# A fused attention and feed-forward kernel: a new order for its first seven chunks and its last four passes

## The chip, the core and the metric

The kernel runs on one core of a Trainium2 chip. A core has TensorE (PE, with its weight loads PEld), VectorE (DVE), ScalarE (ACT), GpSimd (POOL) and SyncE (SP), each with a queue of its own that it works off in order, and 16 DMA engines that they share. The metric is the time of one execution in device microseconds, the median of several runs.

## The reference

For 8 batches, 8 heads, 576 positions and head width 64, with a decay g = 1 - 2^(-5-h) of head h, and the feed-forward part on all 4608 tokens:

```python
scores = scale * np.matmul(q, k.transpose(0, 1, 3, 2))
Dmat = np.where(rel >= 0, gamma[:, None, None] ** rel[None, :, :], 0.0)
ret = scores * Dmat[None, :, :, :]
x = np.matmul(ret, v)            # then heads side by side: 4608 x 512
...
h = x @ w_in                     # 512 x 1024
e = np.exp(h - h_max)
sm = e / (np.sum(e, axis=-1, keepdims=True) + 1e-09)
solu = h * sm
mu = np.mean(solu, axis=-1, keepdims=True)
var = np.mean((solu - mu) ** 2, axis=-1, keepdims=True)
ln = (solu - mu) / np.sqrt(var + 1e-06) * g_ln
return ln @ w_out                # 1024 x 512
```

## The kernel before

The tokens are cut into 36 chunks of 128 rows. Chunks come in four groups of nine: the four full chunks of two batches, alternating, then one chunk that holds the last 64 positions of both. The decay is folded into q and v, so attention is causal linear attention: within a chunk a masked product, between chunks a running state per batch.

A step is a small function that issues one chunk's share of work on one engine. A token such as `eq:2:a` in a string means step `eq` for chunk base + 2, on ACT (`v` is DVE, `g` is POOL). The steps are, in the order in which a chunk goes through them:

- `ld`: three loads (q, k, v; 256 KB each) on SP. `cq`, `ck`, `cv`: q, k, v to 16 bits, q and v scaled.
- `tq`: 8 transposes of q and k into PSUM (PE); `eq`: their copy to SBUF. `sc`: scores (PE); `mk`: the mask on them (DVE, two instructions).
- `kv`: the chunk's share of the state (PE); `ad`: added to the state (DVE); `dk`, `d3`: decayed copies (POOL).
- `av`, `fs`: the attention's output from within the chunk and from the state (PE); `ex`: its copy (xT).
- `m1`: h = x w_in, eight products of 128x512 (PE), or in four pieces `mr` of two. `mx`: the row maximum (DVE); `xp`: the exponential (ACT); `so`: h times it and its sum, into u (DVE); `ce`: mean taken off (DVE); `sq`: sum of squares (ACT); `rt`: one over the root (POOL).
- `tu`: 8 transposes of u (PE); `eu`: their copy uT. `m2`: eight products with w_out (PE). `st`: scaling on ACT and the store on SP.

`li` and `lo` load w_in and w_out in four pieces each, `wi` and `wo` convert them in eight. The steps that begin with h do the last chunk in halves. `wu:0:n` issues n products of a tile of zeros, 128x512, into a PSUM tile that nobody reads.

Nothing is planned at run time: the string START is issued, then LOOP once for each i from FIRST on, then END, and each engine works its instructions off in that order, waiting on semaphores where an operand or a buffer isn't ready. Before, FIRST is 4, LOOP runs for i = 4 to 34, and END does the rest. One pass of LOOP carries m1 of chunk i, m2 of chunk i - 2, scores of chunk i + 2 and loads of chunk i + 6. In PSUM, h has a ring of two; all other tiles share four banks, which the string BANKS deals out in the order of their allocation, so that a step can wait for the reader of another tile that held its bank before.

Of the kernel before, what the change touches and what calls it, by code (L numbers as in the profile page):

```python
# [16 lines left out]

FIRST = 4  # L20
START = """
c1:0 ld:1 li:3 ld:0 ck:0:v li:2 li:1 cq:1:g li:0 cv:1:v ck:1:a cq:0:g wu:0:8 tq:1 ld:3 wu:0:15
kv:1 wi:2:0:v wi:0:0:a eq:1:v ld:2 tq:0 wi:1:1:g cv:0:v wi:3:1:a wu:0:6 sc:1 eq:0:v wi:3:0:a
mk:1 wu:0:3 sc:0 ld:4 kv:0 wi:1:0:v c2:0 lo:0 ad:1 ck:3:a wu:0:1 av:1 ad:0 lo:3 wi:2:1:a mk:0
cq:3:g fs:1 dk:1 tq:3 ex:1:a dk:0 d3:1 wu:0:2 mr:1:3 cq:2:g eq:3:a d3:0 cv:3:v lo:1 mr:1:2
cv:2:g lo:2 ck:2:a wi:0:1:v av:0 kv:3 mr:1:0 sc:3 fs:0 ld:5 cq:4:g ad:3 tq:2 mr:1:1 mk:3
ex:0:a mr:0:2 mr:0:1 kv:2 av:3 mx:1 eq:2:a sc:2 ad:2 dk:3 d3:3 cv:4:g d3:2 mk:2 mr:0:0 mr:0:3
av:2 fs:3 mx:0 fs:2 xp:1 dk:2 wo:0:g ck:4:a ex:2:a tq:4 wo:4:g so:1 kv:4 wu:0:2 m1:2 xp:0
eq:4:a so:0 ce:0 ld:6 wu:0:1 tu:0 ld:7 cq:5:g ce:1 ld:8 ex:3:a ad:4 wo:7:a wo:6:a wo:3:a
wo:2:v sq:1 sc:4 mx:2 m1:3 tu:1 wo:1:a mk:4 eu:0:v av:4 xp:2 wo:5:a ck:5:g cv:5:v tq:5 fs:4  # L30
eq:5:v sq:0 eu:1:a mx:3 rt:1 m2:0 rt:0 cq:6:g so:2 m2:1 st:0 ex:4:a cq:7:g sc:5 ck:6:v cv:6:g
ce:2 xp:3 ld:9 st:1 mk:5 ck:7:g
"""
LOOP = """
tu:-2 so:-1 tq:2 dk:0 d3:0 eq:2:a eu:-2:a ce:-1 m1:0 kv:1 ad:1 av:1 sc:2 mx:0 sq:-2 mk:2 fs:1
ex:1:a rt:-2 cq:4:g xp:0 ld:6 m2:-2 st:-2 cv:3:v ck:4:g
"""
END = """
sq:-2 tu:-2 hm:0:0 eu:-2:a so:-1 ce:-1 hx:0:0 hm:0:1 hx:0:1 hp:0:1 tu:-1 hp:0:0 m2:-2 eu:-1:v
ho:0:1 rt:-2 ho:0:0 m2:-1 sq:-1 rt:-1 hc:0 ht:0:0 hq:0:0:a ht:0:1 hq:0:1:v he:0:0:a st:-2  # L40
he:0:1:v st:-1 h2:0:0 rt:0 h2:0:1 hw:0:0:a hw:0:1:v
"""

BANKS = """
012302210201313202132013203200310210302312032103210231023120312032103213021302310231032103213021
302310231032103213021302310231032103201320130213021032103201320130213021032103201320130213021032
10312031201320132103210312031201320132103210312031201320132013231001
"""


# [25 lines left out]
def kernel(  # L76
# [38 lines left out]
    NCH = len(chunks)  # L115
# [37 lines left out]
    def ld(n):  # L153

        for key, src in (("qf", q), ("kf", k), ("vf", v)):
            dst = load.tile([P, H, D], FP, name=key)
            for pp, b, s0 in rows(n):
                m = pp.stop - pp.start
                nc.sync.dma_start(  # L159
                    out=dst[pp], in_=src[b, :, s0 : s0 + m, :].rearrange("h p d -> p h d")  # L160
                )
            T[key, n] = dst

    def scaled(n, key, out, table, engine):
        dst = half.tile([P, H, D], F16, name=out)
        engine.tensor_tensor(  # L166
            out=dst, in0=T.pop((key, n)), in1=table.unsqueeze(2).to_broadcast([P, H, D]),
            op=ALU.mult,
        )
        T[out, n] = dst  # L170
# [48 lines left out]
    def mk(n):  # L219

        i = 1 if chunks[n][1] == 4 else 0
        m = tris[:, i : i + 1].to_broadcast([P, 4, P])
        T["ret", n] = []
        for e, s in enumerate(T.pop(("sc", n))):
            r = att.tile([P, 4, P], F16, name=f"ret{e}")
            nc.vector.tensor_tensor(out=r, in0=s, in1=m, op=ALU.mult)  # L226
            T["ret", n].append(r)

# [126 lines left out]

    def so(n):

        u = moe.tile([P, DFF], F16, name="u")
        su = tiny.tile([P, 1], FP, name="su")
        nc.vector.scalar_tensor_tensor(  # L360
            out=u, in0=T.pop(("h", n)), scalar=1.0, in1=T.pop(("e", n)), op0=ALU.mult,
            op1=ALU.mult, accum_out=su,
        )
        T["u0", n], T["su", n] = u, su
# [173 lines left out]
    def hw(n, i, e):  # L538

        w = slice(256 * int(i), 256 * int(i) + 256)  # L540
        o_sb = moe.tile([P, 256], FP, tag="o_sbh", name="o_sbh")
        o, rs = T.pop(("ho", n, i)), T["rs", n]
        if e == "a":
            nc.scalar.activation(out=o_sb, in_=o, func=ACT.Copy, scale=rs)
        else:
            nc.vector.tensor_scalar(
                out=o_sb, in0=o, scalar1=rs, scalar2=None, op0=ALU.mult, op1=ALU.bypass
            )
        for queue, (pp, b, s0) in zip((nc.sync, nc.scalar), rows(n)):
            m = pp.stop - pp.start  # L550
            queue.dma_start(out=out[b * S + s0 : b * S + s0 + m, w], in_=o_sb[pp])
# [103 lines left out]
```

## Time and profile before

| | before |
|---|---|
| median of 3 runs | 226.85 us (226.66 to 226.9) |
| the profiled execution's own time | 226.83 us |
| its span, first to last instruction | 225.0 us |
| busy: PE, DVE, ACT, POOL | 211.4, 196.9, 190.9, 163.1 us |
| DMA moved | 42.52 MB, mean 189 GB/s |

Times in the profile are microseconds from the span's start. A row of the timeline has start, duration, engine, line of the kernel, operation, output <- inputs, shapes, count, and in brackets how long the engine had been idle and what it had waited for. Rows of instructions that overlap have durations that add up to more than the distance between their starts. The granted clock (PEclk) is TensorE's, 1.00 being full.

### The profile page before, as it was taken

What the parts mean: (1) busy time and instruction counts of PE and PEld (TensorE: products, weight loads), DVE (VectorE), ACT (ScalarE), POOL (GpSimd) and SP (SyncE); (2) the same over time, 40 slices, a digit from 0 to 9 for tenths busy, and PEclk for the clock granted to TensorE, in tenths of its full rate; (3) what the DMA queues carried; (4) which work ended last, traced back from release to release, by engine and by line L of the source; (5) the groups of instructions that cost most, each with busy time, mean ns of one, the idle gap of its engine ahead of it and who ended that gap; (6) DMA issues with size and microseconds to landing.
All of it is one profiled execution on the core that took longest, in us unless ns stands there. A gap on an engine that the chain in (4) does not pass through costs nothing.

```text
span 225.0 us, 5803 instructions
## 1 busy us (share of the span) xinstructions
PE 211.4 (94%) x2158; PEld 119.0 (53%) x2158; DVE 196.9 (88%) x340; ACT 190.9 (85%) x299; POOL 163.1 (73%) x243
## 2 busy tenths in 40 slices
PE   6778889899999999999999999999999999999982
PEld 2334355455555555555555555555555555555542
DVE  0078788999999999999999999999999999999780
ACT  2107689699999999999999999999999999999972
POOL 2128868798776998887758989887759988883231
PEclk9699999999999999999999999999999999999999
DMA  7999899999999986988898968988898963111204
GB/s 161 246 345 219 220 332 205 225 235 265 258 216 247 238 165 150 262 198 196 182 215 183 216 134 207 240 203 183 204 197 195 196 136 105 47 50 47 93 3 143
DMA packets 121085, 42.52 MB, mean 189 GB/s; under 512 B 114656, under 2 KB 115040, under 8 KB 121056
## 3 DMA queue, kind: packets, MB, share of 16 engines
q1 hardware_dynamic: 119424, 41.82, 81.4%
q10 hardware_dynamic: 1632, 0.32, 0.9%
q8 instruction: 17, 0.28, 0.5%
q14 instruction: 12, 0.10, 0.2%
HBM read 32.70 MB, written 9.44 MB: 187 GB/s over the span
## 4 chain that ended last, share of the span: by engine, by line
PE 62%; SPq 11%; DVE 10%; ACT 6%; POOL 4%; DMA 4%; issue 2%; ACTq 0%; POOLq 0%; DVEq 0%
PE h L335 20%; PE o L418 20%; SPq L159 9%; PE lp L404 5%; PE tp L189 5%; DMA qf<-in_q_dram 4%; PE sc L213 4%; PE x L303 3%; PE kp L237 3%; PE x L288 3%; ACT e L351 2%; DVE nm L345 2%; SPq L580 2%; DVE u L360 2%; SPq L590 1%
## 5 line engine op out<-in xcount | busy, mean ns | idle before, releaser
L418 PE MATMUL o<-w_out,uT 128*128 128x512 f16 x280 | 66.0, 379 | 0.4
L335 PE MATMUL h<-w_in,xT 128*128 128x512 f16 x264 | 62.4, 379 | 0.1
L166 POOL TENSOR_TENSOR q<-qf,small 128x512 f16<-128x512 f32 x36 | 37.7, 1048 | 12.4 <-DMA qf<-in_q_dram 12.4
L226 DVE TENSOR_TENSOR ret<-sc,tris 128x512 f16<-128x512 f32 x72 | 46.0, 679 | 0.4 <-PE sc L213 0.4
L351 ACT ACTIVATE e<-h,nm 128x1024 f32<-128x1024 f32 x35 | 39.1, 1117 | 6.6 <-DVE nm L345 6.2
L360 DVE SCALAR_TENSOR_TENSOR u<-h,e 128x1024 f16<-128x1024 f32 x35 | 42.4, 1212 | 1.9 <-ACT e L351 1.8
L345 DVE TENSOR_REDUCE nm<-h 128x1 f32<-128x1024 f32 x35 | 42.5, 1214 | 0.9 <-PE h L323 0.9
L418 PEld LDWEIGHTS <-uT 128*128 128x128 f16 x280 | 26.1, 98 | 26.7 <-ACT uT L150 0.7
L383 ACT ACTIVATE sq<-u 128x1024 f16<-128x1024 f16 x35 | 37.4, 1069 | 0.0
L335 PEld LDWEIGHTS <-xT 128*128 128x128 f16 x264 | 24.4, 98 | 23.9 <-issue 0.3
L150 ACT COPY qkT<-tp 128x1024 f16<-128x1024 f16 x33 | 33.4, 1012 | 2.5 <-PE tp L189 1.3
L264 POOL TENSOR_TENSOR s<-t,small 128x512 f16<-128x512 f32 x32 | 33.6, 1053 | 0.0
L150 ACT COPY uT<-lp 128x1024 f16<-128x1024 f16 x33 | 33.6, 1018 | 0.0
L395 POOL TENSOR_TENSOR w<-w,ss 128x1 f32<-128x1 f32 x36 | 6.8, 190 | 34.3 <-ACT sq L383 34.0
L150 POOL CAST k<-kf 128x512 f16<-128x512 f32 x30 | 30.9, 1029 | 0.1
L166 DVE TENSOR_TENSOR v<-vf,small 128x512 f16<-128x512 f32 x33 | 29.3, 887 | 1.8 <-DMA vf<-in_v_dram 1.8
L426 ACT ACTIVATE o_sb<-o,rs 128x512 f32<-128x512 f32 x35 | 23.7, 680 | 0.5 <-POOL rs L396 0.5
L404 PEld LDWEIGHTS <-u 128*128 128x128 f16 x280 | 18.3, 98 | 10.1 <-DVE u L374 1.7
L404 PE MATMUL lp<-ident,u 128*128 128x128 f16 x280 | 21.4, 219 | 1.3 <-ACT o_sb L426 1.0
L150 ACT CAST xT<-x 128x512 f16<-128x512 f32 x36 | 21.1, 586 | 1.1 <-PE x L303 1.0
L396 POOL TENSOR_TENSOR rs<-w,mhalf 128x1 f32<-128x1 f32 x36 | 19.8, 549 | 2.9
L276 POOL TENSOR_TENSOR s<-t,small 128x256 f32<-128x256 f32 x24 | 20.3, 844 | 0.0
(68 smaller groups left out, 255.5 us busy)
## 6 DMA issues: line engine op xcount, KB each, us to landing
qf<-in_q_dram SPq DMA_DIRECT2D x32, 256.0 KB, 4.0
kf<-in_k_dram SPq DMA_DIRECT2D x32, 256.0 KB, 4.6
vf<-in_v_dram SPq DMA_DIRECT2D x32, 256.0 KB, 4.9
out_dram<-o_sb SPq DMA_DIRECT2D x32, 256.0 KB, 2.3
w_in<-in_moe_w_in_dram SPq DMA_DIRECT2D x4, 512.0 KB, 5.8
w_out<-in_moe_w_out_dram SPq DMA_DIRECT2D x4, 512.0 KB, 6.0
qf<-in_q_dram SPq DMA_DIRECT2D x8, 128.0 KB, 3.3
kf<-in_k_dram SPq DMA_DIRECT2D x8, 128.0 KB, 3.3
```

Source lines behind the costliest of these rows:

```text
L150: (engine.copy if engine is nc.scalar else engine.tensor_copy)(out=out, in_=in_)
L166: engine.tensor_tensor(out=dst, in0=T.pop((key, n)), in1=table.unsqueeze(2).to_broadcast([P, H, D]), op=ALU.mult,)
L226: nc.vector.tensor_tensor(out=r, in0=s, in1=m, op=ALU.mult)
L264: nc.gpsimd.tensor_tensor(out=s16, in0=t.unsqueeze(2).to_broadcast([P, 4, 2, D]), in1=gd.unsqueeze(3).to_broadcast([P, 4, 2, D]), op=ALU.mult,
L335: nc.tensor.matmul(out=h[:, i * 512 : (i + 1) * 512], lhsT=xT[:, d], rhs=w_in16[:, d, i * 512 : (i + 1) * 512], start=d == 0, stop=d == 3,)
L345: nc.vector.tensor_reduce(out=nm, in_=T["h", n], axis=AX.X, op=ALU.max, negate=True)
L351: nc.scalar.activation(out=e, in_=T["h", n], func=ACT.Exp, bias=T.pop(("nm", n)), accum_out=s)
L360: nc.vector.scalar_tensor_tensor(out=u, in0=T.pop(("h", n)), scalar=1.0, in1=T.pop(("e", n)), op0=ALU.mult, op1=ALU.mult, accum_out=su,)
L383: nc.scalar.activation(out=s, in_=T.pop(("v", n)), func=ACT.Square, accum_out=ss)
L404: nc.tensor.transpose(out=lp[:, c], in_=u[:, c * P : (c + 1) * P], identity=ident)
L418: nc.tensor.matmul(out=o, lhsT=uT[:, c], rhs=w_out16[:, c], start=c == 0, stop=c == NF - 1)
L426: nc.scalar.activation(out=o_sb, in_=T.pop(("o", n)), func=ACT.Copy, scale=T.pop(("rs", n)))
```

## The change

START is rewritten and now covers seven chunks: LOOP begins at i = 7. LOOP itself is the same string, and runs for i = 7 to 31. END is rewritten and covers the last four passes. BANKS is dealt out anew. In START the order of loads is chunk 1, chunk 0, chunk 2, w_in, chunks 4, 3, 5, 6, w_out, chunk 7 and on; before it was chunk 1, a quarter of w_in, chunk 0, the rest of w_in, chunks 3, 2, 4, w_out, chunk 5 and on. Of v, chunks 1, 2, 3, 4, 5, 6 and 7 are converted on POOL; before it was 2, 4 and 6, the others on DVE. Of 38 products of zeros five are left, in one place behind `fs` of chunk 2. In END, the steps of attention and `m1` of chunks 32 to 34 come early, and `m2` of chunks 31 to 34 lie between the last chunk's steps. The rings: loads from 6 to 7, half-width q, k, v from 4 to 5, qkT, ret and xT from 3 to 4, u from 3 to 5, uT from 3 to 5, o_sb from 3 to 4; sq from 3 to 1, the last chunk's own tiles from 3 to 2.

```diff
-FIRST = 4
+FIRST = 7
+STEP = 1
+STOP = 32
 START = """
-c1:0 ld:1 li:3 ld:0 ck:0:v li:2 li:1 cq:1:g li:0 cv:1:v ck:1:a cq:0:g wu:0:8 tq:1 ld:3 wu:0:15
-kv:1 wi:2:0:v wi:0:0:a eq:1:v ld:2 tq:0 wi:1:1:g cv:0:v wi:3:1:a wu:0:6 sc:1 eq:0:v wi:3:0:a
...
+ld:1 c1:0 cq:1:g ck:1:a tq:1 ld:0 ld:2 cq:2:g eq:1:v ck:0:v ck:2:g cv:0:v cq:0:v sc:1 li:3
+mk:1 tq:0 cv:1:g eq:0:v sc:0 kv:0 mk:0 kv:1 av:1 wi:3:0:a tq:2 cv:2:g kv:2 ad:1 eq:2:v
+wi:3:1:g li:2 li:0 d3:1 dk:1 li:1 ad:0 fs:1 av:0 ld:4 ld:3 ex:1:a wi:0:1:v wi:2:1:v wi:2:0:v
+fs:0 mr:1:3 wi:1:1:g d3:0 sc:2 ex:0:v wi:0:0:a mk:2 mr:1:0 mr:1:2 wi:1:0:a mr:1:1 mr:0:0
+cq:4:g ck:4:a ad:2 mr:0:2 dk:0 mx:1 mr:0:1 ld:5 tq:4 eq:4:v mr:0:3 xp:1 d3:2 av:2 sc:4 fs:2
+c2:0 wu:0:5 cv:4:g mx:0 ex:2:a cq:3:g ld:6 so:1 xp:0 ck:3:a ce:1 sq:1 lo:2 kv:4 m1:2 mk:4 so:0
+dk:2 tq:3 av:4 eq:3:a cv:3:g kv:3 fs:4 ex:4:a ck:5:a cq:5:g mx:2 tu:1 cv:5:g tq:5 xp:2 ad:4
+lo:1 eu:1:a sc:3 ad:3 ce:0 m1:4 mk:3 av:3 cq:6:g eq:5:a so:2 ck:6:a dk:3 d3:3 fs:3 mx:4 ex:3:a
+d3:4 cv:6:g sc:5 tq:6 sq:0 d3:6 kv:5 m1:3 ce:2 lo:3 lo:0 eq:6:a tu:2 dk:4 mk:5 ad:5 sc:6 kv:6
+wo:5:g av:5 xp:4 wo:4:a fs:5 mk:6 eu:2:a ld:7 so:4 ex:5:a wo:3:a wo:7:a tu:0 av:6 eu:0:v
+wo:2:a wo:1:a ce:4 d3:5 wo:6:g cq:7:g rt:1 sq:4 wo:0:v rt:0 cv:7:g sq:2 fs:6 rt:4 m1:5 tu:4
+mx:3 ad:6 xp:3 m2:0 eu:4:v ld:8 ld:9 ex:6:a m2:1 dk:5 mx:5 cq:8:g m2:4 ck:7:v so:3 tq:7 dk:6
+ce:3 tu:3 xp:5 st:0 m1:6 kv:7 so:5 sq:3 eq:7:v ck:8:v eu:3:v sc:7 ad:7 ce:5 ld:10 st:1 mx:6
+ld:11 st:4 tq:8 rt:2 ld:12 cv:8:v eq:8:a mk:7 m2:2 m2:3 ck:9:a sc:8 xp:6 rt:3 st:2 av:7 cq:9:g
+mk:8 cq:10:g fs:7 st:3 ex:7:a ck:10:v cv:9:g
 """
...
 END = """
...
+d3:-3 dk:-3 so:-4 cv:0:g tq:-1 m1:-3 eq:-1:a d3:-2 kv:-2 av:-2 ad:-2 sq:-5 sc:-1 fs:-2 mk:-1
+tq:0 ex:-2:a tu:-5 eq:0:a mx:-3 eu:-5:a m1:-2 kv:-1 ce:-4 mx:-2 xp:-3 av:-1 fs:-1 ex:-1:a
+so:-3 m2:-5 sc:0 kv:0 ad:-1 ce:-3 dk:-2 xp:-2 mk:0 so:-2 rt:-5 m1:-1 av:0 dk:-1 sq:-4 mx:-1
+st:-5 sq:-3 fs:0 ex:0:a tu:-3 rt:-4 tu:-4 hm:0:0 eu:-4:a ce:-2 hm:0:1 eu:-3:a xp:-1 tu:-2
+rt:-3 hx:0:0 m2:-3 hx:0:1 hp:0:0 eu:-2:v m2:-4 hp:0:1 st:-3 so:-1 ce:-1 sq:-2 ho:0:1 ho:0:0
+tu:-1 rt:-2 d3:-1 m2:-2 hc:0 sq:-1 eu:-1:v ht:0:1 st:-4 ht:0:0 rt:-1 hq:0:0:v m2:-1 he:0:0:v
+he:0:1:a hq:0:1:a st:-2 st:-1 rt:0 h2:0:0 hw:0:0:a h2:0:1 hw:0:1:v ad:0
 """
...
-            dst = load.tile([P, H, D], FP, name=key)
+            dst = load.tile([P, H, D], FP, name=key, bufs=7)
...
-        u = moe.tile([P, DFF], F16, name="u")
+        u = moe.tile([P, DFF], F16, name="u", bufs=5)
...
-        uT = utp.tile([P, NF, P], F16, name="uT")
+        uT = utp.tile([P, NF, P], F16, name="uT", bufs=5)
...
     with tc.manual_schedule():
         run(START, 0)
-        for i in range(FIRST, NCH - 1):
+        for i in range(FIRST, STOP - STEP + 1, STEP):
             run(LOOP, i)
         run(END, NCH - 1)
```

More of the change, by code (lines that the diff above doesn't have):

```diff
@@ L15 @@
 D = 64
-FIRST = 4
+FIRST = 7
+STEP = 1
+STOP = 32
 START = """
-c1:0 ld:1 li:3 ld:0 ck:0:v li:2 li:1 cq:1:g li:0 cv:1:v ck:1:a cq:0:g wu:0:8 tq:1 ld:3 wu:0:15
-kv:1 wi:2:0:v wi:0:0:a eq:1:v ld:2 tq:0 wi:1:1:g cv:0:v wi:3:1:a wu:0:6 sc:1 eq:0:v wi:3:0:a
[L24 to L32, printed above, removed]
+ld:1 c1:0 cq:1:g ck:1:a tq:1 ld:0 ld:2 cq:2:g eq:1:v ck:0:v ck:2:g cv:0:v cq:0:v sc:1 li:3
[13 more added lines that the diff above has]
+mk:8 cq:10:g fs:7 st:3 ex:7:a ck:10:v cv:9:g
 """
@@ L38 @@
 END = """
-sq:-2 tu:-2 hm:0:0 eu:-2:a so:-1 ce:-1 hx:0:0 hm:0:1 hx:0:1 hp:0:1 tu:-1 hp:0:0 m2:-2 eu:-1:v
-ho:0:1 rt:-2 ho:0:0 m2:-1 sq:-1 rt:-1 hc:0 ht:0:0 hq:0:0:a ht:0:1 hq:0:1:v he:0:0:a st:-2
-he:0:1:v st:-1 h2:0:0 rt:0 h2:0:1 hw:0:0:a hw:0:1:v
+d3:-3 dk:-3 so:-4 cv:0:g tq:-1 m1:-3 eq:-1:a d3:-2 kv:-2 av:-2 ad:-2 sq:-5 sc:-1 fs:-2 mk:-1
[5 more added lines that the diff above has]
+he:0:1:a hq:0:1:a st:-2 st:-1 rt:0 h2:0:0 hw:0:0:a h2:0:1 hw:0:1:v ad:0
 """
 BANKS = """
-012302210201313202132013203200310210302312032103210231023120312032103213021302310231032103213021
-302310231032103213021302310231032103201320130213021032103201320130213021032103201320130213021032
-10312031201320132103210312031201320132103210312031201320132013231001
+012301230130120123010230213103210231230231203012303120312013201302130210321032013201302130210321
+032013201302130210321032013201230123021302132013201230123021302132013201230123021302132013203120
+3123012301320132031203123012301320132013021301203123030213013
 """
@@ L164, in scaled @@
     def scaled(n, key, out, table, engine):
-        dst = half.tile([P, H, D], F16, name=out)
+        dst = half.tile([P, H, D], F16, name=out, bufs=5)
         engine.tensor_tensor(
@@ L175, in ck @@
     def ck(n, e="g"):
-        k16 = half.tile([P, H, D], F16, name="k16")
+        k16 = half.tile([P, H, D], F16, name="k16", bufs=5)
         copy(ENG[e], k16, T.pop(("kf", n)))
@@ L194, in eq @@
     def eq(n, e="v"):
-        qkT = att.tile([P, 2, 4, P], F16, name="qkT")
+        qkT = att.tile([P, 2, 4, P], F16, name="qkT", bufs=4)
         tp = T.pop(("tp", n))
@@ L224, in mk @@
         for e, s in enumerate(T.pop(("sc", n))):
-            r = att.tile([P, 4, P], F16, name=f"ret{e}")
+            r = att.tile([P, 4, P], F16, name=f"ret{e}", bufs=4)
             nc.vector.tensor_tensor(out=r, in0=s, in1=m, op=ALU.mult)
@@ L311, in ex @@
     def ex(n, e="a"):
-        xT = att.tile([P, 4, P], F16, name="xT")
+        xT = att.tile([P, 4, P], F16, name="xT", bufs=4)
         copy(ENG[e], xT, T.pop(("xs", n)))
@@ L379, in sq @@
     def sq(n):
-        s = moe.tile([P, DFF], F16, name="sq")
+        s = moe.tile([P, DFF], F16, name="sq", bufs=1)
         ss = tiny.tile([P, 1], FP, name="ss")
@@ L423, in st @@
     def st(n):
-        o_sb = moe.tile([P, DM], FP, name="o_sb")
+        o_sb = moe.tile([P, DM], FP, name="o_sb", bufs=4)
         nc.scalar.activation(
@@ L462, in hp @@
         i = int(i)
-        e = moe.tile([P, 512], FP, tag="eh", name="eh")
+        e = moe.tile([P, 512], FP, tag="eh", name="eh", bufs=2)
         s = tiny.tile([P, 1], FP, tag="sh", name="sh")
@@ L471, in ho @@
         i = int(i)
-        u = moe.tile([P, 512], F16, tag="uh", name="uh")
+        u = moe.tile([P, 512], F16, tag="uh", name="uh", bufs=2)
         su = tiny.tile([P, 1], FP, tag="suh", name="suh")
@@ L502, in he @@
         i = int(i)
-        uT = utp.tile([P, 4, P], F16, tag="uTh", name="uTh")
+        uT = utp.tile([P, 4, P], F16, tag="uTh", name="uTh", bufs=2)
         copy(ENG[e], uT, T.pop(("hlp", n, i)))
@@ L509, in hq @@
         i = int(i)
-        s = moe.tile([P, 512], F16, tag="sqh", name="sqh")
+        s = moe.tile([P, 512], F16, tag="sqh", name="sqh", bufs=2)
         ss = tiny.tile([P, 1], FP, tag="ssh", name="ssh")
@@ L540, in hw @@
         w = slice(256 * int(i), 256 * int(i) + 256)
-        o_sb = moe.tile([P, 256], FP, tag="o_sbh", name="o_sbh")
+        o_sb = moe.tile([P, 256], FP, tag="o_sbh", name="o_sbh", bufs=2)
         o, rs = T.pop(("ho", n, i)), T["rs", n]
```

## The prediction

> **What bounds the kernel now.** I read the page's first two parts, then one answer of the windows, cut where the work changes character, for all instructions and for the zero products (line 558) alone.
>
> ```profile
> span 225.0 us, 5803 instructions
> ...
> PE 211.4 (94%) x2158; PEld 119.0 (53%) x2158; DVE 196.9 (88%) x340; ACT 190.9 (85%) x299; POOL 163.1 (73%) x243
> PEclk9699999999999999999999999999999999999999
> DMA  7999899999999986988898968988898963111204
> ...
> 0.00:11.52 11.52, 8.32 (x29) 3.18 (x30) 0.28 (x2) 1.90 (x2) 2.27 (x6) 0.85 1.02 205
> 11.52:42.84 31.32, 25.99 (x264) 13.33 (x262) 26.10 (x46) 21.07 (x35) 20.47 (x27) 1.00 1.09 261
> 42.84:59.85 17.01, 16.99 (x183) 9.89 (x184) 16.66 (x28) 14.63 (x22) 14.91 (x22) 1.00 1.15 243
> 59.85:195.63 135.78, 135.56 (x1468) 78.86 (x1465) 132.33 (x223) 130.24 (x201) 113.05 (x165) 1.00 0.85 191
> 195.63:213.00 17.37, 17.37 (x176) 9.79 (x173) 15.38 (x28) 16.79 (x29) 8.97 (x16) 1.00 0.13 49
> 213.00:225.00 12.00, 7.15 (x50) 3.94 (x48) 6.11 (x17) 6.28 (x14) 3.45 (x10) 1.00 0.27 87
> ...
> 0.00:11.52 11.52, 7.69 (x21) 2.77 (x22) 0.85 1.02 205
> 11.52:42.84 31.32, 4.94 (x19) 1.45 (x17) 1.00 1.09 261
> ```
>
> The columns are the stretch, its length, busy time of PE, PEld, DVE, ACT, POOL, the granted clock, the DMA share and GB/s; the last two rows are the zero products. Between 59.85 and 195.63 PE is busy 135.56 of 135.78 us and DVE 132.33: the loop is PE's, with DVE 3% behind. The diff doesn't touch what one pass of the loop does. So the change is worth what it does before 59.85 (where the pass of i=7 starts) and after 195.63 (i=32). Before 42.84 PE's real work is only 8.32 + 25.99 - 7.69 - 4.94 = 21.7 us of 42.8, and DVE does nothing until 11.52. Those 21 us are the stock from which a better start could draw. The tail's stock is small: PE is full until 213, and its last product ends at 219.09 + 1.92 = 221.01 (row below), so 8.01 - 7.15 = 0.86 us of waiting lie in it. DMA is at nine tenths or more through most of the first 80 us: a new order of loads can bring the right bytes first, not more bytes.
>
> **The start, by DVE's account.** I take DVE's list up to the statistics product (so) of chunk 6, with which pass i=7 begins on DVE, because DVE is the engine that the start has to fill: it begins last and then has the densest list. Prices are the distances from one start to the next, which hold the overlap.
>
> ```profile
> 50.17 1.21 DVE L360 SCALAR_TENSOR_TENSOR u<-h,e 128x1024 f16<-128x1024 f32 x1
> ...
> 51.43 0.15 DVE L369 TENSOR_SCALAR nmu<-su 128x1 f32<-128x1 f32 x1
> ...
> 52.02 0.42 DVE L252 TENSOR_TENSOR t<-kp,s 128x256 f32<-128x256 f32 x1
> 52.35 1.22 DVE L345 TENSOR_REDUCE nm<-h 128x1 f32<-128x1024 f32 x1
> 53.48 1.28 DVE L226 TENSOR_TENSOR ret<-sc,tris 128x512 f16<-128x512 f32 x2
> 54.68 0.68 DVE L166 TENSOR_TENSOR v<-vf,small 128x512 f16<-128x512 f32 x1
> 55.28 1.22 DVE L360 SCALAR_TENSOR_TENSOR u<-h,e 128x1024 f16<-128x1024 f32 x1
> ...
> 60.75 1.21 DVE L360 SCALAR_TENSOR_TENSOR u<-h,e 128x1024 f16<-128x1024 f32 x1
> ```
>
> So: so 1.26, ce 0.59, ad 0.33, mx 1.13, mk 1.20, cv 0.60; and chunk 6's product starts at 60.75. The other prices, and the landings of data, are in these rows of the timeline:
>
> ```profile
> 6.26 0.62 ACT L150 CAST k<-kf 128x512 f16<-128x512 f32 x1 [2.28 <-DMA kf<-in_k_dram]
> 10.36 1.04 POOL L166 TENSOR_TENSOR q<-qf,small 128x512 f16<-128x512 f32 x1 [5.29 <-DMA qf<-in_q_dram]
> 11.52 0.43 DVE L150 CAST k<-kf 128x512 f16<-128x512 f32 x1 [10.39 <-DMA kf<-in_k_dram]
> 11.86 0.69 DVE L166 TENSOR_TENSOR v<-vf,small 128x512 f16<-128x512 f32 x1
> 13.91 0.43 DVE L150 CAST w_in<-w_in 128x512 f16<-128x512 f32 x1 [1.36 <-DMA w_in<-in_moe_w_in_dram]
> 14.25 0.68 DVE L150 COPY qkT<-tp 128x1024 f16<-128x1024 f16 x1
> 14.85 0.68 DVE L166 TENSOR_TENSOR v<-vf,small 128x512 f16<-128x512 f32 x1
> 15.22 0.78 POOL L150 CAST w_in<-w_in 128x512 f16<-128x512 f32 x1 [3.82 <-DMA w_in<-in_moe_w_in_dram]
> 16.63 1.66 ACT L150 CAST w_in<-w_in 128x512 f16<-128x512 f32 x3 [9.75 <-DMA w_in<-in_moe_w_in_dram]
> 17.89 1.04 POOL L166 TENSOR_TENSOR q<-qf,small 128x512 f16<-128x512 f32 x1 [1.67 <-DMA qf<-in_q_dram]
> 23.80 0.62 ACT L150 CAST k<-kf 128x512 f16<-128x512 f32 x1 [2.23 <-DMA kf<-in_k_dram]
> 33.81 0.47 DVE L600 TENSOR_SCALAR w_out<-w_out,g 128x512 f16<-128x512 f32 x1
> 34.19 1.04 POOL L605 TENSOR_TENSOR w_out<-w_out,g 128x512 f16<-128x512 f32 x1 [2.27 <-DMA w_out<-in_moe_w_out_dram]
> 37.66 3.87 PE L418 MATMUL o<-w_out,uT 128*128 128x512 f16 x16
> ```
>
> ck and wi are 0.34 (11.52 to 11.86, 13.91 to 14.25), eq 0.60 (14.25 to 14.85), wo 0.47; eu is priced as eq (same size), ex and cq as cv. Before, DVE does up to 60.75: 9 mk, 7 mx, 6 so, 6 ce, 8 ad, 7 cv, 3 eq, 2 ck, 3 wi, 1 eu, 1 wo = 10.8 + 7.9 + 7.6 + 3.5 + 2.6 + 4.2 + 1.8 + 0.7 + 1.0 + 0.6 + 0.5 = 41.2 us from 11.52, so it stood idle 60.75 - 11.52 - 41.2 = 8.0. After, the same mk, mx, so, ce, ad, wi and wo, but 2 cv, 1 cq, 5 eq, 4 ck, 3 eu, 1 ex (seven v conversions move to POOL, copies of qkT and uT come over from ACT): 42.5 us.
>
> It starts earlier: chunk 1's k lands at 6.26 as now, its cast ends at 6.9, its transposes about 7.35, and eq of chunk 1, which now heads DVE's list, runs at 7.45 instead of ck of chunk 0 at 11.52: 4.1 us. What it then waits for, I walk by hand. Landings: a quarter of w_in takes 1.3 to 1.4 us (13.91, 15.22, 16.63), and a third of a chunk 1.16 (10.36 to 11.52) to 1.48 (four of them from 17.89 to 23.80). Without the quarter that stood before it, chunk 0's q lands at 10.36 - 1.3 = 9.05, k 10.2, v 11.4; chunk 2 by 14.9; w_in from 16.2 to 20.1; chunk 4's k at 22.8 (1.35 a piece). PE's prices are these, at full clock:
>
> ```profile
> 60.30 0.45 PE tp L189 x8
> 60.75 1.73 PE h L335 x8
> 62.82 0.33 PE sc L213 x8
> ...
> 7.16 5.09 PE L558 MATMUL w<-warm 128*128 128x512 f16 x15
> 13.30 1.46 PE L558 MATMUL w<-warm 128*128 128x512 f16 x6
> ```
>
> The idle times, as they follow: 2.1 until k of chunk 0; 0.8 until its v; 0.8 until sc of chunk 0 (half clock); 1.35 until tq of chunk 2, whose PSUM bank is the one that mk of chunk 0 frees, with av of chunk 1 before it; 0.6 until k of chunk 4 is cast and transposed; from there DVE is fed, since seven chunks' attention and two h buffers keep a product or a reduction ready. Later gaps: 0.8 for sc of chunk 6 (behind eq and sq on ACT), 0.7 for the exponential of chunk 3 (ACT has four pieces of w_out and two squares before it), 0.55 for kv of chunk 7, 0.7 for sc of chunk 8 behind two m2 (1.73 each, as m1). Sum 8.4. So DVE reaches chunk 6's product at 7.45 + 42.5 + 8.4 = 58.35, 2.4 us ahead of 60.75. PE follows: its tq of chunk 9 takes the bank that mk of chunk 8 frees (58.2), and m1 of chunk 7 starts near 58.85 against 60.75, 1.9 ahead. I take **2.0**. Bounds: if a third of a chunk takes 1.48 throughout, chunk 0 and 2 come 1.9 later, all of it idle: 0.1 gained. If the four late gaps (2.75) vanish: 4.8.
>
> Off the path: w_out now lands after seven chunks instead of five (by the same rates near 41.7, when now it is all in at about 34), so the first m2 comes at 44 instead of 37.66; PE has m1 of five chunks and the attention of seven to do until then, and takes up the lost m2 in a row while DVE runs ahead. That cover gone, each us of lateness costs one on PE. POOL's seven v conversions stand behind q conversions that wait for DMA; they delay kv, which has slack. Larger rings (loads 7, half 5, u 5, uT 5) cost no instruction; loads can issue one chunk further ahead, worth nothing while DMA is full. SP now holds stores of chunks 0, 1, 4 between loads 9 to 12; chunk 10's k, needed last by DVE at 58, lands about 55.5.
>
> **The zero products.** 33 of 38 go: 12.6 us of PE time, at present all in PE's waits, worth nothing by themselves. They do hold the clock: 15 of them from 7.16 took 5.09 us (0.34 each), the 6 from 13.30 took 1.46 (0.24), and the granted clock is 0.85 over the first 11.52 us and 1.00 after. Afterwards PE has almost nothing between 9.0 and 12.6, then is dense from 14.4. In m1 such a product takes 1.73 / 8 = 0.216; if a slow one takes twice that, (5.09 - 15 x 0.216) / 0.216 = 8.6 of the 15 were slow, which is 3.7 us. I take the same delay and so full clock near 18.5, already in the walk; it is where m1's first pieces start.
>
> The Trainium skill, page "TensorE: Matmul & The Clock Gate", Part 1, says that the array idles at half clock, speeds up after about 3.4 us of sustained work and falls back after an idle window of that length; by it the gate would open near 18, and the sum would not change. Its Part 4 says that transposes don't count as such work. No run here shows that yet; by it the dense stretch is thinner, and the gate opens later, which is the second rival.
>
> **The tail.** The four last passes put attention and m1 first and keep m2 of chunks 31 to 34 as filler between the last chunk's steps.
>
> ```profile
> 219.09 1.91 PE L532 MATMUL oh<-w_out,uTh 128*128 128x256 f16 x16 [0.67 <-DVE uTh L150]
> ```
>
> That 0.67 is the longest wait that the filler covers: m2 of chunk 34 stands behind the last transposes, not before them. The cap is the 0.86. Against it, DVE's list for the four passes is about as long as now, with new waits (tu of chunk 30 for mk of chunk 34's bank, near 0.65), and hc comes about when PE gets there. Between -0.4 and 0.86, I take **0.4**.
>
> **Sum.** The profiled execution is 226.83 us (span 225.0 and 1.83 around it), the median 226.85; so 226.83 - 2.0 - 0.4 = 224.4.
>
> **Rivals.** (1) The landings are as slow as 1.48 a third and the late gaps stay: start 0.1, tail 0.3, 226.4. For it: DMA is full, and the order puts three chunks of short rows before w_in. Against: the first pair took 1.16. Chance 0.15. (2) Slower: without the zero products the clock stays at half until m1's first run at 27. PE then has between 18.8 and 27: eight pieces of m1 (0.43 each), tq 0.45, two sc, av, fs and five zero products (0.24 each) = 3.4 + 0.45 + 1.3 + 1.2 = 6.4 us at full clock, in 8.2; doubled, 12.8, so all that follows comes 4.6 later: 226.83 - 2.4 + 4.6 = 229.0. Each us of half clock in that stretch costs 4.6 / 8.2 = 0.56, so it turns slower than before when full clock comes after 18.8 + 2.4 / 0.56 = 23. For it: PE's busy time in that stretch is small products and transposes. Against: gaps under a microsecond didn't close the gate between 11.52 and 42.84 (25.99 busy of 31.32, clock 1.00). Chance 0.18. (3) The late gaps close, since ACT has room: start 4.0, 222.4. Chance 0.12. My forecast has 0.55, its own range 223.2 to 225.9.
>
> From case (1) I give 0.06 to each of faster and same and 0.03 to slower; from (2) 0.17 to slower, 0.01 to same. A measurement of this kernel tells about 0.2%, 0.45 us, from no change. Faster 0.55 + 0.12 + 0.06 = 0.73, same 0.07, slower 0.20. The range leaves out part of (2) and (3): 222.2 to 228.4.
>
> **What would show it.** DVE's first eq at 7 to 8 us; DVE's idle time up to chunk 6's product near 8.4 and that product near 58.3; granted clock 1.00 from 18 or 19; m2 of chunk 0 near 44; last product about 2.4 earlier than 221.01. The prediction is wrong if the clock is below 1 after 23, if w_out lands after 44, or if PE shows idle time inside the loop.

## The result and the profile after

| | before | after |
|---|---|---|
| median of 6 runs | 226.84 us (226.66 to 226.93) | 223.43 us (222.6 to 224.0) |
| the profiled execution's own time | 226.83 us | 223.33 us |
| its span | 225.0 us | 221.5 us |

The ratio is 0.9845, interval [0.9825, 0.9866]: 3.4 us faster, where 2.4 were forecast. From the first two parts of the page of the kernel after:

```profile
span 221.5 us, 5624 instructions
...
PE 203.6 (92%) x2125; PEld 117.8 (53%) x2125; DVE 196.2 (89%) x343; ACT 186.6 (84%) x294; POOL 163.8 (74%) x245
...
PEclk9999999999999999999999999999999999999999
```

PE lost 7.8 us of busy time: the zero products fell from 12.6 to 1.2 us, and all the rest together rose by 3.6, largely since products up to 19.4 us now run slowly (below). DVE's busy time is the same within 0.7 us and its share rose to 89%. The windows of the kernel after, cut at chunk 6's so and near the last passes (columns as in the prediction):

```profile
7.41:58.56 51.15, 44.02 (x449) 25.48 (x450) 44.55 (x77) 34.08 (x56) 39.17 (x53) 1.00 1.08 251
58.56:192.76 134.20, 134.00 (x1449) 77.72 (x1447) 129.78 (x222) 128.62 (x198) 110.38 (x162) 1.00 0.87 198
192.76:205.00 12.24, 11.75 (x132) 6.52 (x130) 11.57 (x19) 10.80 (x20) 9.25 (x16) 1.00 0.12 45
205.00:217.60 12.60, 12.59 (x96) 7.41 (x93) 9.52 (x25) 11.23 (x21) 3.79 (x12) 1.00 0.18 67
```

The loop is PE's as before (134.00 busy of 134.20), so its passes cost what they did. The chain of waits gives the two ends of it, m1 of chunk 7 and m1 of chunk 32. First the chain of the kernel after, then that of the kernel before, whose first end (60.75) the prediction shows:

```profile
57.89 1.73 PE h L345 x8
...
193.20 1.73 PE h L345 x8
```

```profile
196.52 1.73 PE h L335 x8
```

Before, the stretch is 196.52 - 60.75 = 135.77; after, 193.20 - 57.89 = 135.31. The 0.46 is the transposes of u of chunk 30 (0.45), which the new END issues behind m1 of chunk 32 and not ahead of it. So the account is: m1 of chunk 7 is 60.75 - 57.89 = **2.86** earlier; from the end of m2 of chunk 29 (195.63 before, 192.76 after) to the last product (221.01, 217.60) it is 25.38 against 24.84, **0.54**; what follows the last product is 3.99 against 3.90, 0.1. The sum is 3.5, the difference of the spans.

The start on DVE, timeline of the kernel after; all waits up to chunk 6's so (the last row), and the instructions that took unusually long:

```profile
7.41 0.69 DVE L160 COPY qkT<-tp 128x1024 f16<-128x1024 f16 x1 [6.29 <-PE tp L199]
9.89 0.43 DVE L160 CAST k<-kf 128x512 f16<-128x512 f32 x1 [1.79 <-DMA kf<-in_k_dram]
11.09 0.69 DVE L176 TENSOR_TENSOR v<-vf,small 128x512 f16<-128x512 f32 x1 [0.77 <-DMA vf<-in_v_dram]
...
14.90 1.29 DVE L236 TENSOR_TENSOR ret<-sc,tris 128x512 f16<-128x512 f32 x2 [0.70 <-PE sc L223]
...
17.29 0.69 DVE L160 COPY qkT<-tp 128x1024 f16<-128x1024 f16 x1 [0.77 <-PE tp L199]
...
23.34 0.69 DVE L160 COPY qkT<-tp 128x1024 f16<-128x1024 f16 x1 [0.52 <-PE tp L199]
...
26.53 1.35 DVE L384 TENSOR_SCALAR u<-u,nmu 128x1024 f16<-128x1024 f16 x1
...
38.73 1.29 DVE L236 TENSOR_TENSOR ret<-sc,tris 128x512 f16<-128x512 f32 x2 [0.27 <-PE sc L223]
...
46.63 1.22 DVE L370 SCALAR_TENSOR_TENSOR u<-h,e 128x1024 f16<-128x1024 f32 x1 [0.37 <-ACT e L361]
...
51.70 0.42 DVE L262 TENSOR_TENSOR t<-kp,s 128x256 f32<-128x256 f32 x1 [0.34 <-POOL s L274]
...
56.29 1.29 DVE L236 TENSOR_TENSOR ret<-sc,tris 128x512 f16<-128x512 f32 x2 [0.64 <-PE sc L223]
57.49 1.15 DVE L160 CAST k<-kf 128x512 f16<-128x512 f32 x1
58.56 1.21 DVE L370 SCALAR_TENSOR_TENSOR u<-h,e 128x1024 f16<-128x1024 f32 x1
```

The list begins at 7.41 and chunk 6's so comes at 58.56. In brackets behind the first row stand nine waits, 6.2 us in all, and all nine are ones that the walk had named. (The one at 51.70 is put down to POOL; chunk 7's kv, which the walk had named for it, ended within 0.1 us of that.) The same timeline's rows of PE and of POOL, for the clock, chunk 4's transposes, the last wait before the loop, the first m2, chunk 9's transposes, the tail, and two of POOL's products; between them, ACT's conversion of chunk 4's k:

```profile
12.44 0.61 PE L199 MATMUL tp<-ident,q 128*128 128x128 f16 x4 [3.67 <-DVE q L176]
...
17.97 1.03 PE L333 MATMUL h<-w_in,xT 128*128 128x512 f16 x2
...
19.37 3.05 PE L333 MATMUL h<-w_in,xT 128*128 128x512 f16 x12
...
22.91 0.40 PE L199 MATMUL tp<-ident,k 128*128 128x128 f16 x4 [0.27 <-ACT k L160]
...
39.47 0.41 PE L298 MATMUL x<-ret,v 128*64 128x128 f16 x8 [0.53 <-DVE ret L236]
...
43.38 5.34 PE L428 MATMUL o<-w_out,uT 128*128 128x512 f16 x24
...
57.28 0.39 PE L199 MATMUL tp<-ident,q 128*128 128x128 f16 x4
...
204.23 0.38 PE L298 MATMUL x<-ret,v 128*64 128x128 f16 x7 [0.38 <-DVE ret L236]
...
215.68 1.91 PE L542 MATMUL oh<-w_out,uTh 128*128 128x256 f16 x16
```

```profile
22.24 0.62 ACT L160 CAST k<-kf 128x512 f16<-128x512 f32 x1 [1.75 <-DMA kf<-in_k_dram]
```

```profile
26.55 1.04 POOL L274 TENSOR_TENSOR s<-t,small 128x512 f16<-128x512 f32 x1
...
57.32 1.04 POOL L274 TENSOR_TENSOR s<-t,small 128x512 f16<-128x512 f32 x1
```

PE's last wait ahead of the loop is the 0.53 at 39.47: the output of chunk 5 (av) needs the PSUM bank that the first half of chunk 6's mask frees (38.73 on DVE). From there to m1 of chunk 7 PE is busy for all of the 18.42 us. In the kernel before, the last such wait stands at 42.84:

```profile
42.84 0.62 PE L404 MATMUL lp<-ident,u 128*128 128x128 f16 x8 [0.98 <-ACT o_sb L426]
```

From there to 60.75 are 17.91 us, and PE is busy for all but a few hundredths of them. So 3.37 us are gained up to PE's last wait, and 0.51 is lost behind it, which makes the 2.86.

The last wait of the tail of before, 0.67 ahead of the last product, is gone: 215.68 has no bracket. What is left is the 0.38 at 204.23, where chunk 35's av waits for chunk 35's mask. (In this timeline a group that PE runs without a gap begins up to 0.2 earlier than its piece of the chain.)

### The profile page after: what moved, and what is told of

Its sections match the earlier page's. It is cut to its first block, busy times and chain, and to the rows that moved or that the text cites. A ratio compares the mean times of both kernels' runs of the same rounds, so it can differ in the third digit from the quotient of the medians.

```text
span 221.5 us, 5624 instructions
## 1 busy us (share of the span) xinstructions
PE 203.6 (92%) x2125; PEld 117.8 (53%) x2125; DVE 196.2 (89%) x343; ACT 186.6 (84%) x294; POOL 163.8 (74%) x245
## 4 chain that ended last, share of the span: by engine, by line
PE 81%; DVE 6%; SPq 6%; DMA 4%; issue 1%; ACT 0%; DVEq 0%
PE o L428 27%; PE h L345 24%; PE lp L414 7%; PE tp L199 6%; PE sc L223 5%; SPq L169 5%; PE x L313 4%; DMA kf<-in_k_dram 4%; PE x L298 4%; PE kp L247 3%; DVE ret L236 1%; DVE u L370 1%; DVE nm L355 1%; DVE u L384 1%; SPq L590 1%
## 5 line engine op out<-in xcount | busy, mean ns | idle before, releaser
L176 POOL TENSOR_TENSOR q<-qf,small 128x512 f16<-128x512 f32 x35 | 36.9, 1056 | 12.1 <-DMA qf<-in_q_dram 11.9
L160 ACT COPY qkT<-tp 128x1024 f16<-128x1024 f16 x31 | 31.4, 1012 | 3.0 <-PE tp L199 2.2
L160 ACT COPY uT<-lp 128x1024 f16<-128x1024 f16 x30 | 30.4, 1018 | 0.3 <-PE lp L414 0.3
L160 POOL CAST k<-kf 128x512 f16<-128x512 f32 x26 | 27.4, 1054 | 0.2 <-DMA kf<-in_k_dram 0.2
L199 PE MATMUL tp<-ident,q 128*128 128x128 f16 x144 | 14.6, 226 | 8.8 <-POOL q L176 5.1
L406 POOL TENSOR_TENSOR rs<-w,mhalf 128x1 f32<-128x1 f32 x36 | 20.6, 571 | 2.8
L160 ACT CAST xT<-x 128x512 f16<-128x512 f32 x35 | 20.5, 585 | 2.5 <-PE x L313 2.3
L176 DVE TENSOR_TENSOR v<-vf,small 128x512 f16<-128x512 f32 x27 | 21.9, 812 | 0.8 <-DMA vf<-in_v_dram 0.8
```

The costliest lines, as they stand in the source:

```text
L160: (engine.copy if engine is nc.scalar else engine.tensor_copy)(out=out, in_=in_)
L176: engine.tensor_tensor(out=dst, in0=T.pop((key, n)), in1=table.unsqueeze(2).to_broadcast([P, H, D]), op=ALU.mult,)
L199: nc.tensor.transpose(out=tp[:, i, hp], in_=s2[:, hp * P : (hp + 1) * P], identity=ident)
```

## The experiments

The theory: the gain is DVE's, whose list begins 4.1 us earlier and is fed soon after; the zero products and the rings are bystanders, and the tail adds half a microsecond. Rivals: the gain comes from PE's 33 products less; from the rings; from the order of loads alone, whatever the steps do. Times are medians, each with the kernel before on the same chip: 226.88 for the first four kernels, 226.82 for the next four, 226.73 for the last four.

**The start and the tail apart.** The first has the new START and rings with the old END (loop to 34); the second the old START, 38 zero products included, with the new END and rings.

```diff
-STOP = 32
+STOP = 35
 END = """
-d3:-3 dk:-3 so:-4 cv:0:g tq:-1 m1:-3 ...
+sq:-2 tu:-2 hm:0:0 eu:-2:a so:-1 ce:-1 ...
```

> New order of the first seven chunks and new rings, with the old last four passes (LOOP runs to i = 34 again). Theory (the start gives 2.9 of the 3.4 us, since DVE begins 4.1 us earlier): 226.84 - 2.9 = 223.9, and m1 of chunk 7 at 57.9 as in the changed kernel. Rival (the new tail carries half or more): 225.2 or above.

> Old first chunks with all their zero products, new last four passes, new rings. Theory: the tail gives 0.5, so 226.3. Rival (tail carries half or more): 225.2 or below. Second rival (the larger rings do it, wherever the order): 224 or below.

The start alone: 224.37 us, ratio 0.9887 [0.9867, 0.9908], 2.51 gained. The tail alone: 226.13, 0.9976 [0.996, 0.9991], 0.75 gained. The sum, 3.26, lies between the whole change's 3.41 in the result and 2.98 in a later session (below): as far as this noise tells, the two parts don't hang on each other. The start alone missed its 223.9 and its m1 of chunk 7 at 57.9, which came at 58.83. Chunk 4's k was there at 23.16 instead of 22.24, 0.92 later, and PE's last wait ended at 40.41, 0.94 later; from there to m1 are again 18.42 us. The last product of the start alone, and of the tail alone, in their timelines:

```profile
217.07 1.91 PE L539 MATMUL oh<-w_out,uTh 128*128 128x256 f16 x16 [0.67 <-DVE uTh L157]
```

```profile
218.63 1.91 PE L539 MATMUL oh<-w_out,uTh 128*128 128x256 f16 x16
```

With the old END the 0.67 stands there again; with the new one it is gone, though the start is the old one.

**The zero products.** Put back: 8 ahead of the first transposes and 15 ahead of chunk 0's, in the changed kernel. Taken away: 30 of the 38, in the kernel before.

```diff
-ld:1 c1:0 cq:1:g ck:1:a tq:1 ...
-mk:1 tq:0 cv:1:g ...
+ld:1 c1:0 cq:1:g ck:1:a wu:0:8 tq:1 ...
+mk:1 wu:0:15 tq:0 cv:1:g ...
```

> The changed kernel with 23 zero products put back: 8 ahead of the first transposes, 15 between the scores of chunk 1 and the transposes of chunk 0, where PE idles. Theory (the zero products lay in waits, and without them PE only runs at half clock until about 19.5): full clock from about 11 to 12, the waits for sc of chunk 0 and tq of chunk 2 get shorter by 0.8 together, and as the next waits are for DMA landings (w_in, k of chunk 4) little of it remains: 223.0 to 223.5. Rival (33 products less is 12.6 us less PE work, and that is the gain): slower by 23/33 of the 3.4 us, 225.8. Rival (half clock costs the start dearly): 222.5 or below.

> The kernel before with one zero product at each of its eight places, 8 instead of 38. Theory (they lie in waits, and hold the clock): no gain, and by half clock until about 20 up to 1 us lost: 226.8 to 227.8. Rival (their 12.6 us of PE time is on the path): 224 to 225.

Put back they gained nothing: 224.17, 0.9884 [0.9864, 0.9904]. Taken away from the kernel before: 226.96, 1.0009 [0.9982, 1.0035]. So PE's smaller number of products is not the gain. The expected 223.0 to 223.5 was missed for a reason that the timeline of the first one shows:

```profile
9.28 5.53 PE L569 MATMUL w<-warm 128*128 128x512 f16 x15
14.87 0.38 PE L200 MATMUL tp<-ident,q 128*128 128x128 f16 x4
```

The 15 ran at 0.37 us each and held up chunk 0's transposes to 14.87, where the changed kernel has them at 12.44; after that products ran at full speed (those 8 transposes in 0.6 us instead of 1.0), which gave part of it back. A smaller dose was tried, 8 and 8; and one with the gain vector's load, made of 4-byte pieces, moved from 2 us to behind chunk 4's k conversion.

```diff
-    nc.scalar.dma_start(out=gln, in_=moe_g_ln.rearrange("(c p) -> p c", p=P))
+    def gl(_):
+        nc.scalar.dma_start(out=gln, in_=moe_g_ln.rearrange("(c p) -> p c", p=P))
```

> The changed kernel with 8 zero products ahead of the first transposes and 8, not 15, between the scores of chunk 1 and the transposes of chunk 0, so that they end when q of chunk 0 is converted (12.3). Theory (half clock until 19.5 costs DVE 0.6 in two waits, and the later waits for w_in and for k of chunk 4 swallow part of it): chunk 6's product 0.0 to 0.6 before 58.56, 222.8 to 223.4. Rival (half clock costs nothing, since DMA sets the early stretch): as the changed kernel, within 0.2.

> As the one before, and the load of the gains (4 KB in pieces of 4 bytes, on ACT's queue) moved from 2 us to behind the cast of k of chunk 4, and its scaling behind q of chunk 5. Theory (DMA sets the early stretch, and 1024 small pieces cost it time there): k of chunk 0 lands 0.3 to 0.8 before 9.9 and all that follows with it; 222.4 to 223.0. Rival (small pieces on another queue cost nothing): as the one before.

Both miss: 224.6, 0.9924 [0.9896, 0.9952], and 223.48, 0.986 [0.9843, 0.9878]; the changed kernel in the same session (below) 223.75. The profiled run of the first is its slowest of six (226.35; the others took 225.54 or less), and two of its windows and a row of ACT's timeline show what was late in it:

```profile
15.00:17.50 2.50, 1.86 (x44) 1.49 (x45) 2.13 (x4) 1.10 (x2) 2.50 (x4) 0.96 1.04 416
17.50:20.00 2.50, 2.50 (x20) 1.00 (x18) 1.75 (x6) 0.62 (x1) 1.09 (x2) 0.50 1.09 345
```

```profile
23.62 0.62 ACT L161 CAST k<-kf 128x512 f16<-128x512 f32 x1 [2.84 <-DMA kf<-in_k_dram]
```

The clock opened early and shut again: granted 0.50 from 17.5 to 20, just when m1's first pieces run; and chunk 4's k came at 23.62, where the changed kernel has it at 22.24. With the gain's load out of the way chunk 0's k was there 0.4 earlier, but chunk 4's k again only at 23.14. DVE's timeline of that kernel:

```profile
9.51 0.43 DVE L161 CAST k<-kf 128x512 f16<-128x512 f32 x1 [1.40 <-DMA kf<-in_k_dram]
...
24.25 0.69 DVE L161 COPY qkT<-tp 128x1024 f16<-128x1024 f16 x1 [1.82 <-PE tp L200]
```

What is won at 10 us is lost at 24, in one wait of 1.82 for chunk 4, instead of 0.52: PE's last wait ended at 39.73, against 40.00 in the changed kernel of the same session. Why that k lands at 22.2 in one run and 23.6 in another, though SP issues its load at 14.0 or 14.1 in both, stays open.

**The order of loads.** All steps as changed, but w_in is loaded as before: a quarter ahead of chunk 0, the rest ahead of chunk 2. (The other loads move forward in the string too, but keep their order on SP.)

```diff
-ld:1 c1:0 cq:1:g ck:1:a tq:1 ld:0 ld:2 ...
+ld:1 c1:0 li:3 ld:0 li:2 li:1 li:0 ld:2 ld:4 ld:3 ld:5 ld:6 lo:2 lo:1 lo:3 lo:0 cq:1:g ...
```

> The changed kernel with the loads of w_in ahead again (chunk 1, a quarter of w_in, chunk 0, the rest of w_in, then chunk 2), all else the same. Theory (what the start gains is the early landing of chunks 0 and 2): q, k and v of chunk 2 land near 18 to 20 instead of 12.4 to 14.9, its qkT copy on DVE runs near 22 instead of 17.3, everything behind it is some 4 us later: 227 to 228. Rival (DMA moves the same bytes by 24 either way, and DVE's order alone makes the gain): within 0.5 of the changed kernel, 223.4 to 223.9.

230.63, 1.0173 [1.0146, 1.02]: 7 us worse than the change, and slower than before, the way that was expected but by some 3 us more than the 227 to 228. Its timeline, POOL, then PE, then DVE:

```profile
17.71 1.04 POOL L176 TENSOR_TENSOR q<-qf,small 128x512 f16<-128x512 f32 x1 [12.48 <-DMA qf<-in_q_dram]
...
19.46 2.04 POOL L176 TENSOR_TENSOR v<-vf,small 128x512 f16<-128x512 f32 x2
```

```profile
20.56 0.42 PE L247 MATMUL kp<-v,k 128*64 128x64 f16 x8 [3.83 <-POOL v L176]
```

```profile
21.02 0.42 DVE L260 COPY t<-kp 128x256 f32<-128x256 f32 x1 [3.33 <-PE kp L247]
22.41 0.69 DVE L160 COPY qkT<-tp 128x1024 f16<-128x1024 f16 x1 [0.97 <-PE tp L199]
```

Each engine works its queue in order here: POOL has chunk 2's q ahead of chunk 1's v, which had long been loaded; chunk 2's q now comes behind all of w_in, POOL stands 12.48 us for it, PE 3.83 for the v, DVE 3.33 for PE, and chunk 2's copy runs at 22.41 instead of 17.29. m1 of chunk 7 comes 6.0 us later, at 63.92; where the last us arises is not settled. The kernel before had that order of loads with other steps.

**The conversions of v.** Chunks 1, 3, 5 and 7 back on DVE.

```diff
-cv:1:g ... cv:3:g ... cv:5:g ... cv:7:g
+cv:1:v ... cv:3:v ... cv:5:v ... cv:7:v
```

> The changed kernel with v of chunks 1, 3, 5 and 7 converted on DVE again instead of POOL. Theory (DVE fills the start, and each 0.6 us on its list counts): four conversions are 2.4 us of DVE work; the first, of chunk 1, falls into a wait, so 1.8 is left: 225.2. Rival (POOL is what the early chunks wait for, since it stands on q of chunk 2 before v of chunk 1): 223.4 or faster.

226.57, 0.9984 [0.9961, 1.0007]: with four conversions of 0.60 back on DVE the whole gain of the start is gone, and more than the 1.8 that were expected. Chunk 6's so came at 61.44, 2.88 later. Rows of PE, a window, and a new wait of DVE's:

```profile
31.02 0.32 PE L247 MATMUL kp<-v,k 128*64 128x64 f16 x8 [1.36 <-DVE v L176]
...
33.94 3.29 PE L345 MATMUL h<-w_in,xT 128*128 128x512 f16 x8
```

```profile
34.00:36.00 2.00, 2.00 (x6) 0.66 (x6) 2.00 (x4) 2.00 (x3) 2.00 (x3) 0.50 0.95 337
```

```profile
37.26 1.23 DVE L355 TENSOR_REDUCE nm<-h 128x1 f32<-128x1024 f32 x1 [0.85 <-PE h L345]
```

PE waits 1.36 us for DVE's v at 31.02; then the granted clock falls to 0.50, and m1 of chunk 4 takes 3.29 us instead of 1.90, for which DVE waits in its turn. So DVE's list counts here, but in this execution up to 1.4 of the 2.88 us are the clock's, and how much of the median is the clock no run shows.

**The rings.** The changed kernel with the larger rings back at their old sizes (but uT's, left at 5); the kernel before with the new ones; and, after the first missed, the changed kernel with o_sb's ring alone at its old 3, beside the changed kernel once more.

```diff
-        o_sb = moe.tile([P, DM], FP, name="o_sb", bufs=4)
+        o_sb = moe.tile([P, DM], FP, name="o_sb")
```

> The changed kernel with all rings at their old sizes but uT's, which stays at 5. Theory (the rings cost and save nothing but let the order be): the changed order holds four u at once (chunks 4, 3 and 5 between so and sq), so up to 0.5 is lost, 223.4 to 223.9; with the loads ring at 6 nothing else changes. Rival (the rings make the gain): 225 or above.

> The kernel before with the new ring sizes (loads 7, half 5, attention 4, u 5, uT 5, o_sb 4) and nothing else. Theory: no wait in the old order is for a ring, 226.8, within 0.3. Rival (larger rings let loads run ahead): 225.5 or below.

> The changed kernel with the ring of o_sb at 3 again, all other rings as changed. Theory (with old rings the fourth and fifth store of the start waited 1.96 us for an o_sb tile whose store stood in SP's queue behind loads, and PE 1.49 us behind that): the whole loss of the old rings comes back, 225.0 to 226.2, with a wait of ACT for a store near 58 us. Rival (another ring, u's or the loads', made that loss): within 0.5 of the changed kernel.

> The changed kernel once more, on the chip of the three others, so that tenths can be told: 223.4 by all theories, ratio 0.985 to the kernel before.

Old rings: 226.18, 0.996 [0.9928, 0.9993], in runs from 224.4 to 227.9, where at most 0.5 above the change was expected. New rings alone: 227.08, 1.0009 [0.9993, 1.0026], nothing. o_sb's ring alone at 3: 224.97, 0.9924 [0.9904, 0.9943]; the changed kernel beside it 223.75, 0.9876 [0.9852, 0.99]. So o_sb's fourth tile is worth 1.2 us in this order and nothing in the old one. The timeline with three tiles, SP's queue, then ACT, then PE:

```profile
49.20 1.11 SPq L441 DMA_DIRECT2D out_dram<-o_sb  x1
...
53.60 0.93 SPq L441 DMA_DIRECT2D out_dram<-o_sb  x1
```

```profile
57.80 0.69 ACT L436 ACTIVATE o_sb<-o,rs 128x512 f32<-128x512 f32 x1 [1.91 <-DMA out_dram<-o_sb]
```

```profile
58.54 0.61 PE L414 MATMUL lp<-ident,u 128*128 128x128 f16 x8 [1.45 <-ACT o_sb L436]
```

The new START issues five stores close together, the first four each in SP's queue behind the loads of a chunk. The second was issued at 53.60; ACT's fifth write of the ring needs that tile and stood until 57.80, and PE's transposes of u needed the PSUM bank that this write frees. m1 of chunk 7 came 1.2 us later than in the changed kernel beside it (59.43 against 58.26 in the timelines). With the old rings the profiled run has the same wait (1.96). Its median is another 1.2 higher, in runs that lie 3.4 us apart; whether another ring has a share in that is not settled. Nothing that was run is faster than the change by more than the spread of its runs.

## Why the prediction was right

**What held.** The gain lies in the start, for the greater part, and in DVE's list the forecast was close: it was to begin at 7.45, stand idle 8.4 us and reach chunk 6's so at 58.35; it began at 7.41 and got there at 58.56. The 0.21 is two errors that nearly cancel. The waits, item by item, predicted against measured: k of chunk 0 2.1 and 1.79; its v 0.8 and 0.77; its scores 0.8 and 0.70; chunk 2's transposes 1.35 and 0.77; chunk 4's 0.6 and 0.52; scores of chunk 6 0.8 and 0.27; exponential of chunk 3 0.7 and 0.37; kv of chunk 7 0.55 and 0.34; scores of chunk 8 0.7 and 0.64: 2.2 us less. The work took 51.15 - 6.17 = 45.0, not 42.5. Of these 2.5, ce of chunk 1 (1.27 from its start to the next, where its price has some 0.4 for it) and ck of chunk 10 (1.07 against 0.34) make 1.6; and each wait also ends the overlap of two instructions, which prices from start to start leave out (a pair of mk lasts 1.29 and was priced 1.20), nine times 0.09. The same prices were short before: from 11.52 to 60.75 DVE was busy for 43.66 us, not 41.2, so it stood idle for 5.6, not 8.0. As both lists were short by about as much, the difference between them stood: DVE's own gain was put at 2.4 and was 60.75 - 58.56 = 2.19.

**The step that was off** is the one from DVE to PE: m1 of chunk 7 was put at 58.85, 1.9 ahead, and the gain taken as 2.0; it was 57.89, 2.86 ahead. The step had chunk 9's transposes wait until DVE was through with mk of chunk 8, at 58.2. They didn't wait for it: the bank was free when the first of mk's two instructions ended, at about 57.0, and PE, busy without a gap since 39.47, came to them at 57.28. What sets m1 of chunk 7 in the profile is PE's own queue from 39.47 on, 18.42 us, the same distance as in the start alone (40.41 to 58.83) and in the changed kernel's second profile (40.00 to 58.42). So PE parts from DVE's list at the first half of chunk 6's mask, 19 us before the list's end, and DVE's slow ck of chunk 10 (1.15) cost PE nothing.

**What sets the 39.47** the prediction had only as one wait among nine. The chain of waits runs back from there over PE and DVE to the copy of chunk 4's transposes (23.34), and from that to the landing of chunk 4's k, converted by ACT at 22.24, for which PE waited 0.27 and DVE 0.52. So by this chain DVE could have got through the copies and conversions ahead of 22.8 half a microsecond later at no cost, and the list's start at 7.41 decides little by itself. Before, the chain from PE's last wait at 42.84 has no DVE in it: it runs back over ACT, with its writes of o_sb, and over POOL to chunk 5's q, which was loaded behind w_out and is now loaded ahead of it. This is its row of the chain before:

```profile
35.39 1.04 POOL q L166
```

No run moves that load alone. Shown by runs is that the new START makes the gain, that it needs the early chunks ahead of w_in, and that the zero products, or the rings with the old order, don't make it; the path through the start is read from the chains. That the two errors on DVE cancelled, and that DVE's end lay within a us of PE's, is luck.

**The tail**, 0.4, measured 0.54 in the profiled pair and 0.75 by its own experiment; the 0.67 is covered as argued. The new wait is not the one that was named (transposes of u of chunk 30, 0.65): PE has no gap there. It is chunk 35's av for chunk 35's mask, with 0.38.

**Also as said:** m2 of chunk 0 at 43.38 (predicted 44), so w_out came in time; the loop without idle time; the zero products worth nothing by themselves. (The 12.6 us that the prediction gives to the 33 that go are those of all 38; the five that stay take 1.2.)

**The clock** was worse than assumed without a price: at 17.97 two products of m1 took 0.5 us each and at 19.37 twelve took 0.25, so full speed came at about 19.4, not 18.5 (the prediction's own 14.4 and 3.7 make 18.1). That is far from the 23 at which the second rival turns slower, and its 229.0 didn't come. The granted clock doesn't show it: it reads 1.00 throughout, and only the products' durations tell. PE was busy for 5.17 of the 5.18 us from 14.26 to 19.44. The Trainium skill, "TensorE: Matmul & The Clock Gate", Part 1, has the clock open after about 3.4 us of sustained work; here it took longer. The Trainium skill, same page, Part 4, says that transposes don't count as such work. The eight in this stretch fill 0.9 us of it (16.24 to 17.18), by an estimate from that page's 3.4 about half of the difference; no run here tests it. The first rival needed thirds of 1.48 us throughout: the waits for chunk 0 and 2 came out shorter than forecast. The third rival's late gaps did close by 1.1 of its 2.75, but the extra us doesn't come from there: DVE reached chunk 6's so no earlier than forecast.

**Missed** was one ring: "cost no instruction" was true, "worth nothing" was argued for the loads and taken over for all. The stores between loads 9 and 12 stood in the prediction, but not who waits for their tile: with three tiles of o_sb the changed order loses 1.2 us.

## What to carry to other kernels

Price a new order of a pipeline's start on the engine that has to be filled: when its list begins, its work at prices from the trace, and its waits named one by one. Then look for the last landing that this list waits for, since what comes earlier on it may have slack, and for the last point at which the bottleneck still needs that engine, since from there its own queue decides. Change the order of loads and of steps together: here the new steps with the old place of w_in were slower than the kernel before, by 1.7%. For every ring ask which queue releases its tiles: a store behind loads on the same queue can hold a tile, its PSUM bank and then TensorE.

## What the runs showed of the hardware

- Some of DVE's instructions from SBUF to SBUF stretch when they meet a product on POOL. In the changed kernel ce of chunk 1 ran from 26.53 to 27.88, POOL's product from 26.55 to 27.59; ck of chunk 10 from 57.49 to 58.64, POOL's from 57.32 to 58.36. Both ended 0.28 to 0.29 behind POOL's, and elsewhere in that trace they take 0.49 and 0.43. The Trainium skill, "GPSIMD Engine Reference", Specifications, has POOL share its SBUF interface with VectorE, with contention when DVE runs in a two-port mode; the two rows agree, and no experiment was made on it. So a conversion moved from DVE to POOL may not be quite free for DVE.
- The clock can shut again in a stretch of small products. With 8 + 8 zero products the granted clock was 0.96 from 15 to 17.5, with PE busy 1.86 of those 2.5 us in transposes and attention, and 0.50 from 17.5 to 20; no gap on PE in the 5 us before was over 0.8 us. With v on DVE it was 1.00 from 30 to 32, with PE busy 0.97 of those 2 us, and 0.50 from 34 to 36. With 8 + 8 zero products and the gain's load moved it stayed at 1.00 from 15 to 20, so it does not always shut there.
